# One block with adaptive norm, cached attention and a gated feed-forward: first pair's statistics on ScalarE, plane sums and scaling on GpSimd, first product copied, norm steps in order, seven split weights

## The chip, the cores and the metric

The kernel runs on one core of one Trainium2 chip. The core has five engines that are told apart in the profile: PE (TensorE, with its weight loads as PEld), DVE (VectorE), ACT (ScalarE), POOL (GpSimd) and SP (SyncE, which here issues DMAs). The metric is device microseconds of one execution; the time given is the median of the runs.

## The reference, cut to what matters

```python
x = A_x                                                   # 2048 tokens, 576 channels
sa, ca, ga, sb, cb, gb = silu(c) @ w_mod                  # six rows of 576
h = layernorm(x) * (1 + ca) + sa
x = x + ga * attention(h, k_cache, v_cache, wq, wo)       # 32 heads of 128, 16 kv heads, last 512 keys
h = layernorm(x) * (1 + cb) + sb
x = x + gb * ((sigmoid(h @ w_gate) * (h @ w_up)) @ w_down)  # 4608 hidden channels
```

Everything is float32. A product of two float32 matrices is made of three matmuls: each operand is split into a high part that PE takes whole and the remainder (`hi` and `lo`), and hi*lo, lo*hi and hi*hi are summed in PSUM (function `three`).

## The kernel before

Tokens are cut into four blocks of 512 (`xs[0..3]`, 128 partitions x 4 tiles x 576). There are three stages.

**Attention (0 to 1437 us).** A loop over 512 steps (`n`, one step for each tile of 128 queries of a head) issues projection matmuls (`qp`), scores (`st<-kt,qt`), transposes of the probabilities (`st<-ident,pp`) and value products (`ot<-ptt,vs`). DVE takes the negated maximum (`neg`), subtracts the low parts (`ptt`, `qt`) and scales the output (`ov<-ot,rb`); ACT makes the exponentials (`pp`) and high parts. Work for later stands beside it: `at_n(n, ...)` puts a function at a step. In this way the norm of blocks 2 and 3 (`norm_block`, L648), which the second half of the attention reads, is spread over steps near the middle, and the weights of the later stages are prepared in the background (`bg_load`, `bg_sums`, `bg_split`, `bg_store`): they are read into "rooms", which are the tiles of `xs` not in use, summed on POOL, split on ACT and POOL and written to DRAM. A loop at L812 plans the steps of these jobs by when a room comes free. `shift_cols` (L855) turns a row into columns by PE transposes. For the last two blocks of queries the reciprocal sums are spread over partitions by `spread_rs` (four diagonal tiles `dg` on DVE) and `spread_mm` (four matmuls with ones, then an ACT copy to `rb`).

**Output projection (1437 to some 1820 us).** 32 "visits", one for each tile of 128 tokens, pair of blocks and group of weights; the blocks of a pair are multiplied together by a scheme of seven products in place of eight. A visit has seven stages (`STAGES`) of 12 matmuls of 128x288. Its left operands are four planes `vr` loaded from DRAM and three sums of them (`vt`, made by `v_sum`, one of which overwrites a plane); each is split by `v_split` into `vh` (ACT the high part, DVE the low part). After each stage DVE adds the PSUM bank (tags a, b, c) onto `x`. With visit 24 (`DONE0`) the first pair of blocks is complete, and from there its second norm runs beside the visits: `ln_stats` and the chain of small DVE steps in `ln_chain`, then `early_norm` on ACT, `early_scale` on POOL or DVE, `early_sum` on DVE.

**Feed-forward (some 1820 to 3079 us).** 36 units of hidden channels for each pair of blocks; a unit has seven products (`product`, L1162; `a<-hc,sw`, `b<-hc,sw`, `c<-hc,sw`) of seven matmuls of 128x512, and between them the down products (`w<-wh,hl`). Weights come ready from DRAM (`wsc`) by `load_w` into `sr` (4 buffers) and are split by `split_w` into `sw` (5 buffers): ACT copies the high part, and POOL and DVE take turns in subtracting the low part. Each product issues at its end one `split_w` and one `load_w`, and only then is its PSUM bank copied (`keep`). S2's product leaves bank a, ACT copies it to `g1` (`g<-a`), and S3's product, one further on, goes into the same bank. At units 4, 9, 14 and 19 `late_tile` makes the second norm of the second pair: DVE and POOL work, and five DMAs (`put`) that write the result to DRAM from SP's queue.

**Order.** A scheduler may reorder instructions that are not pinned; `pin` and `keep_order` hold an instruction to the program's order. Each engine then runs its own list in order. SP issues loads and stores in one list too: a store that waits for its data holds up each load behind it.

Of the kernel before, what the change touches and what calls it, by code (L numbers as in the profile page):

```python
# [44 lines left out]
def adaln_block_kernel(ctx: ExitStack, tc: tile.TileContext, x, k_cache, v_cache, wq, wo, w_gate, w_up, w_down,  # L45
# [146 lines left out]
    def ln_chain(b, both):  # L192
        sl = slice(0, 2) if both else slice(b % 2, b % 2 + 1)
        mv, y, v, a = [z[:, sl] for z in LN[b][2]]
        yi, vi = y.bitcast(I32), v.bitcast(I32)
        ops = [lambda: nc.vector.tensor_scalar(v, mv[:, :, :, 1], EPS, None, op0=OP.add),
# [6 lines left out]
        ops += [lambda: nc.vector.scalar_tensor_tensor(a, mv[:, :, :, 0], -1.0, y, op0=OP.mult, op1=OP.mult)]  # L203
# [281 lines left out]
    def expo(n):  # L485
# [159 lines left out]
    for b in range(NB):  # L645
        at_n(N - 48 + 4 * b, load_x, b)

    def norm_block(b, n_stats, n_apply, n_t, step, sc_, sh_, mul, add):  # L648
# [4 lines left out]
        for k in range(12):  # L653
            at_n(n_stats + TPB + k, ln_some, b, False, k, k + 1)
# [3 lines left out]
    norm_block(2, n1 - 35, n1 - 19, n1 - 14, 2, scale, shift, nc.gpsimd, nc.gpsimd)  # L658
# [10 lines left out]
    EX = {}  # L669
# [10 lines left out]
    def early_scale(t, b):  # L680
        h = xs[b][:, t, :]
        (nc.vector if b else nc.gpsimd).tensor_mul(h, h, rows2["scale"])

    def early_sum(t, k):
        if k == 0 and t % 2 == 0:
            for c in (T1, T2, T4):
                EX[c, t // 2] = hp.tile([P, 2, D2], F32, tag="ts", name="ex", bufs=6)
# [131 lines left out]
    while jobs or wide:  # L819
# [10 lines left out]
        for r in rooms:  # L830
            free[r] = n + {"ab": 10, "tail": 13}.get(kind, 12)
        at_n(n, bg_load, k, rooms)
        for part in range(2):
            at_n(n + 4 + part, bg_sums, k, part)
            if kind != "ab":
                at_n(n + 6 + part, bg_split, k, part)
        for part in range(4 if kind == "tail" else 1):
            at_n(n + (7 if kind == "ab" else 8) + part, bg_store, k, part)
        due = max(due, n - 2) + {"ab": 4.6, "tail": 7.6}.get(kind, 5.9)

# [13 lines left out]

    def shift_cols():  # L855
        row = rows2["shift"]
        p = ps_wo()
        for half in range(2):
            e = wp.tile([P, 4, TQ], F32, tag="hd", name="hd", bufs=1)
            n0 = half * D2  # L860
            pin(nc.gpsimd.tensor_copy(e, row[:, None, n0 + 2 * P : n0 + D2].to_broadcast([P, 4, TQ])))
            for k in range(3):
                src = row[0:1, n0 + k * P : n0 + (k + 1) * P] if k < 2 else e.rearrange("p q d -> p (q d)")[0:1]
# [4 lines left out]
    at_n(110, shift_cols)  # L868
# [43 lines left out]
    def v_sum(v, k):  # L912
# [3 lines left out]
        eng = nc.vector if v > DONE0 and k % 2 else nc.gpsimd  # L916
        if k == 0:
            eng.tensor_add(VSUM[v, 0], raw[2], raw[3])
        elif k == 1:
            eng.tensor_sub(raw[2], raw[0], raw[2])  # L920
        elif k == 2:
            eng.tensor_sub(VSUM[v, 2], VSUM[v, 0], raw[0])
        else:
            eng.tensor_sub(VSUM[v, 3], raw[1], VSUM[v, 2])
# [71 lines left out]
    def stage_half(pair, c, i):  # L996
        t = hp.tile([P, 2, D2], F32, tag="ts", name="ts", bufs=6)
# [61 lines left out]
    def split_w():  # L1059
# [4 lines left out]
        t = fpool["s"].tile([P, 5, P], F32R, tag="sw", name="sw", bufs=5)  # L1064
# [122 lines left out]
    def late_load(t):  # L1187
        LATE[t] = [hp.tile([P, 2, D2], F32, tag="ts", name=n, bufs=6).rearrange("p a d -> p (a d)")
# [31 lines left out]
    def beside(v, s):  # L1220
# [14 lines left out]
        if DONE0 - 4 < v <= DONE0 and s in (0, 2):  # L1235
            ln_stats(s // 2, v - DONE0 + 3)
# [4 lines left out]
        if 3 <= k < 10:  # L1241
            ln_some(0, True, 2 * (k - 3), 2 * (k - 2), True)
# [22 lines left out]
    for v in range(VISITS):  # L1265
        q, pair, t = VISIT[v]
        banks = {}
        for s, (plane, combo, tag, row, col) in enumerate(STAGES):
            fresh = tag not in banks
            if fresh:  # L1270
                banks[tag] = fpsum(tag, 2 if tag == "a" else 1, [P, BLK])[:, :D2]
            p = banks[tag]
# [5 lines left out]
            dst = xs[2 * pair + row][:, t, col * D2 : (col + 1) * D2]  # L1278
            nc.vector.tensor_add(dst, p, dst)
# [162 lines left out]
```

## Time and profile before

| | us |
|---|---|
| median of 3 runs | 3082.25 |
| lowest and highest run | 3081.03 and 3084.95 |
| the profiled execution: its own time | 3081.02 |
| its span in the profile | 3079.0 |
| PE busy | 3022.5 |
| DVE, ACT, POOL busy | 2190.9, 1680.2, 1641.9 |

All engines' instructions are put down to one line, L36, because a helper records each of them; so the profile is read by tile names. A row of the timeline gives start, duration, engine, operation, the tiles written and read, the shape and, in brackets, the idle time ahead of it with what ended it. A row of the windows gives the stretch, its length, then the busy time of PE, PEld, DVE, ACT and POOL with their counts, the granted TensorE clock, the share of the DMA engines and GB/s.

### The profile page before, as it was taken

What the parts mean: (1) busy time and instruction counts of PE and PEld (TensorE: products, weight loads), DVE (VectorE), ACT (ScalarE), POOL (GpSimd) and SP (SyncE); (2) the same over time, 40 slices, a digit from 0 to 9 for tenths busy, and PEclk for the clock granted to TensorE, in tenths of its full rate; (3) what the DMA queues carried; (4) which work ended last, traced back from release to release, by engine and by line L of the source; (5) the groups of instructions that cost most, each with busy time, mean ns of one, the idle gap of its engine ahead of it and who ended that gap; (6) DMA issues with size and microseconds to landing.
All of it is one profiled execution on the core that took longest, in us unless ns stands there. A gap on an engine that the chain in (4) does not pass through costs nothing.

```text
span 3079.0 us, 49150 instructions
## 1 busy us (share of the span) xinstructions
PE 3022.5 (98%) x16651; PEld 2600.9 (84%) x16651; DVE 2190.9 (71%) x3872; ACT 1680.2 (55%) x3358; POOL 1641.9 (53%) x1534
## 2 busy tenths in 40 slices
PE   8999999999999999999999999999999999999998
PEld 6888788878888888887999888888888888888887
DVE  6666666677666666667888987666666876666667
ACT  5666666656667676554334454444544545444542
POOL 2334368644577773212555327666655666555654
PEclk9999999999999999999999999999999999999999
DMA  4687778766777777654546535555555564554453
GB/s 124 182 199 213 193 235 249 218 183 185 194 250 249 249 238 185 174 172 169 204 160 263 214 125 173 170 158 163 166 148 142 159 187 135 148 146 142 135 159 100
DMA packets 468795, 558.72 MB, mean 181 GB/s; under 512 B 51136, under 2 KB 421056, under 8 KB 459584
## 3 DMA queue, kind: packets, MB, share of 16 engines
q1 hardware_dynamic: 467408, 555.06, 60.1%
q8 instruction: 132, 2.16, 0.3%
q14 instruction: 119, 0.97, 0.1%
q10 hardware_dynamic: 1136, 0.53, 0.1%
HBM read 388.04 MB, written 167.41 MB: 180 GB/s over the span
## 4 chain that ended last, share of the span: by engine, by line
PE 87%; DVE 5%; POOL 3%; issue 2%; ACT 1%; DMA 1%; SPq 0%; POOLq 0%; ACTq 0%; DVEq 0%
PE a L36 19%; PE st L36 17%; PE qp L36 13%; PE w L36 12%; PE ot L36 11%; PE c L36 10%; PE b L36 5%; DVE x L36 1%; POOL x L36 1%; DVE vh L36 1%; POOL hl L36 0%; PE wo L36 0%; POOL vs L36 0%; DVE neg L36 0%; ACT pp L36 0%
## 5 line engine op out<-in xcount | busy, mean ns | idle before, releaser
L36 DVE TENSOR_TENSOR x<-w,x 128x288 f32<-128x288 f32 x980 | 435.6, 454 | 299.7 <-PE w L36 295.8
L36 PE MATMUL a<-hc,sw 128*128 128x512 f32 x2016 | 584.9, 395 | 9.2 <-POOL sw L36 5.2
L36 DVE TENSOR_REDUCE neg<-st 128x1 f32<-128x512 f32 x512 | 352.7, 689 | 281.1 <-PE st L36 281.1
L36 ACT ACTIVATE ptt<-st 128x512 fp32r<-128x512 f32 x512 | 306.2, 598 | 394.3 <-PE st L36 393.9
L36 PE MATMUL ot<-ptt,vs 128*128 128x512 f32 x1536 | 487.2, 425 | 2.9 <-DVE ptt L36 2.9
L36 PE MATMUL qp<-hTm,wa 128*128 128x512 f32 x1536 | 446.1, 399 | 4.9 <-DVE qt L36 2.8
L36 PE MATMUL st<-kt,qt 128*128 128x512 f32 x1536 | 443.0, 395 | 1.4 <-ACT pp L36 1.4
L36 DVE TENSOR_TENSOR ptt<-st,ptt 128x512 fp32r<-128x512 f32 x512 | 352.2, 688 | 123.4 <-ACT ptt L36 123.0
L36 ACT ACTIVATE sw<-sr 128x384 fp32r<-128x384 f32 x504 | 261.7, 521 | 261.9 <-issue 91.3
L36 PEld LDWEIGHTS a<-hc,sw 128*128 128x128 f32 x2016 | 355.9, 188 | 51.0 <-POOL sw L36 6.5
L36 ACT ACTIVATE pp<-st,neg 128x512 f32<-128x512 f32 x512 | 350.8, 685 | 55.6 <-DVE neg L36 55.1
L36 POOL TENSOR_TENSOR sw<-sr,sw 128x256 fp32r<-128x256 f32 x252 | 195.0, 775 | 325.1 <-ACT sw L36 228.9
L36 PEld LDWEIGHTS qp<-hTm,wa 128*128 128x128 f32 x1536 | 284.2, 188 | 74.2 <-DVE qt L36 8.3
L36 PEld LDWEIGHTS w<-wh,hl 128*128 128x128 f32 x1776 | 299.3, 189 | 54.8 <-DVE x L36 6.0
L36 PEld LDWEIGHTS st<-kt,qt 128*128 128x128 f32 x1536 | 288.5, 189 | 66.6 <-ACT pp L36 2.4
L36 PE MATMUL w<-wh,hl 128*128 128x288 f32 x1776 | 332.9, 298 | 3.4 <-DVE x L36 3.3
L36 POOL TENSOR_TENSOR x<-x 128x256 f32<-128x256 f32 (+3 forms) x334 | 246.9, 758 | 152.0 <-DMA x<-in_B_w_up_dram 88.4
L36 PEld LDWEIGHTS st<-ident,pp 128*128 128x128 f32 x2048 | 255.8, 140 | 78.0 <-issue 7.2
L36 PE MATMUL st<-ident,pp 128*128 128x128 f32 x2048 | 307.9, 273 | 9.2 <-DVE rs L36 6.4
L36 PE MATMUL c<-hc,sw 128*128 128x512 f32 x1008 | 303.8, 394 | 0.0
L36 PEld LDWEIGHTS ot<-ptt,vs 128*128 128x128 f32 x1536 | 253.5, 191 | 29.7 <-DVE ptt L36 4.2
L36 POOL TENSOR_TENSOR hl<-vs,hl 128x512 fp32r<-128x512 f32 x139 | 186.7, 1343 | 98.9 <-ACT hl L36 98.9
(211 smaller groups left out, 5107.1 us busy)
## 6 DMA issues: line engine op xcount, KB each, us to landing
sr<-wsc SPq DMA_DIRECT2D x504, 192.0 KB
wh<-dsc SPq DMA_DIRECT2D x144, 288.0 KB
dsc<-x SPq DMA_DIRECT2D x34, 1008.0 KB
vr<-oscr SPq DMA_DIRECT2D x32, 1024.0 KB
rb<-rscr SPq DMA_DIRECT2D x126, 256.0 KB
wsc<-x SPq DMA_DIRECT2D x36, 896.0 KB
oscr<-ov SPq DMA_DIRECT2D x63, 512.0 KB
wosc<-x SPq DMA_DIRECT2D x32, 1008.0 KB
```

Of the source, the lines that this page charges most:

```text
L36: i = got(*args, **kw)
```

## The change

- The small steps of the norm chain of blocks 2 and 3 are pinned, and block 2's statistics and application stand one step later.
- `spread_mm` is one matmul of 128x512 in place of four of 128x128, and stands one step later for the last but one block and two for the last.
- The two POOL copies that `shift_cols` needs are made ahead of it, at steps 100 and 101, into two buffers; the transposes stand at step 106 instead of 110.
- Background jobs hold their rooms one step longer, with the second half of a split and the stores one step later; the last reloads of `x` wait for the rooms.
- In each visit ACT copies the first product's bank into bank b, where the sixth product is then accumulated; the DVE add after the first product goes.
- The first pair's statistics move from DVE's `bn_stats` to ACT: three passes for each tile (a sum, its scaling to the negated mean, and the sum of squares about it), at visits 21 to 24.
- From visit 25 all of `v_sum` is on POOL (two of four were on DVE), and all of `early_scale` too.
- `sw` has seven buffers instead of five, `sr` three instead of four, `ts` four instead of six; two of the sums of `early_sum` lie in `sw` buffers. Three weights are loaded ahead, five are split beside the visits, and unit 1 has one more split and load.

```diff
-    def ln_chain(b, both):
-        sl = slice(0, 2) if both else slice(b % 2, b % 2 + 1)
-        mv, y, v, a = [z[:, sl] for z in LN[b][2]]
+    def chain(first, v, y, a, last):
...
-                at_late(n - 1, spread_mm, b)
+                at_late(n + (0 if b == NBLK - 2 else 1), spread_mm, b)
...
     def spread_mm(b):
         p = ps_qp()
-        for i in range(TPB):
-            nc.tensor.matmul(p[:, i * P : (i + 1) * P], ones, DG[b][:, i], start=True, stop=True)
+        nc.tensor.matmul(p, ones, DG[b].rearrange("p i q -> p (i q)"), start=True, stop=True)
...
-            at_n(n_stats + TPB + k, ln_some, b, False, k, k + 1)
+            at_n(n_stats + TPB + k, ln_some, b, False, k, k + 1, True)
...
-    norm_block(2, n1 - 35, n1 - 19, n1 - 14, 2, scale, shift, nc.gpsimd, nc.gpsimd)
+    norm_block(2, n1 - 34, n1 - 18, n1 - 14, 2, scale, shift, nc.gpsimd, nc.gpsimd)
...
+    def early_stats(b, t):
...
+        pin(nc.scalar.activation(junk, x, AF.Copy, accum_out=sums))
+        pin(nc.scalar.activation(means, sums, AF.Copy, scale=-1.0 / D))
+        pin(nc.scalar.activation(junk, x, AF.Square, bias=means, accum_out=squares))
...
-        (nc.vector if b else nc.gpsimd).tensor_mul(h, h, rows2["scale"])
+        nc.gpsimd.tensor_mul(h, h, rows2["scale"])
...
-            free[r] = n + {"ab": 10, "tail": 13}.get(kind, 12)
+            free[r] = n + {"ab": 10, "tail": 14}.get(kind, 13)
...
-                at_n(n + 6 + part, bg_split, k, part)
+                at_n(n + 6 + 2 * part, bg_split, k, part)
...
+    def shift_ends(half):
+        e = ends2[half] = wp.tile([P, 4, TQ], F32, tag=f"hd{half}", name="hd", bufs=1)
...
-    at_n(110, shift_cols)
+    for half in range(2):
+        at_n(100 + half, shift_ends, half)
+    at_n(106, shift_cols)
...
-        eng = nc.vector if v > DONE0 and k % 2 else nc.gpsimd
...
-            t = fpool["s"].tile([P, 3, P], F32, tag="sr", name="sr", bufs=4)
+            t = fpool["s"].tile([P, 3, P], F32, tag="sr", name="sr", bufs=3)
...
-        t = fpool["s"].tile([P, 5, P], F32R, tag="sw", name="sw", bufs=5)
+        t = fpool["s"].tile([P, 5, P], F32R, tag="sw", name="sw", bufs=7)
...
-            ln_stats(s // 2, v - DONE0 + 3)
+            early_stats(s // 2, v - DONE0 + 3)
...
-            for _ in range(4):
+            for _ in range(3):
                 load_w(True)
-        if k in (36, 39, 42, 45):
+        if k in (35, 38, 41, 44, 46):
             split_w()
             load_w(True)
...
+                if s == 0:
+                    banks["b"] = fpsum("b", 1, [P, BLK])[:, :D2]
...
-            dst = xs[2 * pair + row][:, t, col * D2 : (col + 1) * D2]
-            nc.vector.tensor_add(dst, p, dst)
+            if s == 0:
+                pin(nc.scalar.activation(banks["b"], p, AF.Copy))
+            else:
+                dst = xs[2 * pair + row][:, t, col * D2 : (col + 1) * D2]
+                nc.vector.tensor_add(dst, p, dst)
...
+        if u == 1:
+            split_w()
+            load_w()
```

**Three places in the order of instructions.** The first is DVE's list in the middle of the attention, where the norm of blocks 2 and 3 runs (`ln_a`, `ln_y` are the chain's small tiles, `h` a normed tile). Before:

```order
L36 SCALAR_TENSOR_TENSOR ln_a<-ln_a,ln_v 128x4
L36 SCALAR_TENSOR_TENSOR ln_y<-ln_a,ln_y 128x4
L36 TENSOR_TENSOR ln_a<-ln_y 128x4
L36 SCALAR_TENSOR_TENSOR ln_a<-ln_a,ln_v 128x4
L36 SCALAR_TENSOR_TENSOR ln_y<-ln_a,ln_y 128x4
L36 TENSOR_REDUCE neg<-st 128x1
L36 TENSOR_TENSOR ptt<-st,ptt 128x4x128
```

And with the change, where the same part of block 3's chain stands:

```order
L36 SCALAR_TENSOR_TENSOR ln_y<-ln_a,ln_y 128x4
L36 TENSOR_TENSOR ln_a<-ln_y 128x4
L36 TENSOR_REDUCE neg<-st 128x1
L36 TENSOR_TENSOR ptt<-st,ptt 128x4x128
L36 TENSOR_TENSOR ov<-ot,rb 128x4x128
L36 SCALAR_TENSOR_TENSOR qt<-qp,qt 128x512
L36 TENSOR_REDUCE neg<-st 128x1
L36 TENSOR_TENSOR ptt<-st,ptt 128x4x128
L36 SCALAR_TENSOR_TENSOR ln_a<-ln_a,ln_v 128x4
L36 SCALAR_TENSOR_TENSOR ln_y<-ln_a,ln_y 128x4
L36 TENSOR_REDUCE neg<-st 128x1
```

Five chain steps that stood in one run now stand in runs of two, with the attention's `neg` and `ptt` between.

The second is POOL's list in the visits after the first pair is complete (`x_101` and `x_102` are the first pair's blocks). Before:

```order
L36 TENSOR_TENSOR x_101<-x_101,scale_2199 128x576 x2
L36 COPY te<-x_101 128x256
L36 TENSOR_TENSOR x_101<-x_101,scale_2199 128x576
L36 TENSOR_TENSOR vt<-vr 128x512
L36 TENSOR_TENSOR vt<-vt,vr 128x512
L36 TENSOR_TENSOR x_101<-x_101,scale_2199 128x576
L36 COPY te<-x_101 128x256
```

With the change:

```order
L36 TENSOR_TENSOR x_101<-x_101,scale_2199 128x576
L36 COPY te<-x_101 128x256
L36 TENSOR_TENSOR x_102<-x_102,scale_2199 128x576
L36 TENSOR_TENSOR vt<-vr 128x512
L36 TENSOR_TENSOR x_101<-x_101,scale_2199 128x576
L36 TENSOR_TENSOR vr<-vr 128x4x128
L36 TENSOR_TENSOR x_102<-x_102,scale_2199 128x576
L36 TENSOR_TENSOR vt<-vt,vr 128x512
L36 TENSOR_TENSOR vt<-vr,vt 128x512
L36 TENSOR_TENSOR x_101<-x_101,scale_2199 128x576
```

The scaling of both blocks and four sums of a visit now stand in POOL's list, where there were one block and two sums.

The third is ACT's list in the feed-forward's unit 4, after the first `late_tile` (`v1`, `g0`, `g1` are copies of PSUM banks; numbers tell buffers apart, and the loads of `sr` come from SP in the order of their numbers). Before:

```order
L36 ACTIVATE v1_20550<-c_20445 128x512
L36 ACTIVATE g0_20468<-g0_20468 128x512
L36 ACTIVATE sw_20570<-sr_20466 128x384
L36 ACTIVATE g1_20575<-a_20443 128x512
L36 ACTIVATE sw_20596<-sr_20492 128x384
L36 ACTIVATE sw_20623<-sr_20523 128x384
L36 ACTIVATE g1_20575<-g1_20575 128x512
```

With the change:

```order
L36 ACTIVATE sw_20549<-sr_20470 128x384
L36 ACTIVATE v1_20554<-c_20449 128x512
L36 ACTIVATE g0_20472<-g0_20472 128x512
L36 ACTIVATE sw_20574<-sr_20496 128x384
L36 ACTIVATE g1_20579<-a_20447 128x512
L36 ACTIVATE sw_20600<-sr_20527 128x384
L36 ACTIVATE sw_20627<-sr_20552 128x384
L36 ACTIVATE g1_20579<-g1_20579 128x512
```

The list has the same shape, but each split takes a load one further on; SP's list shows where these loads are issued. Before, the loads on both sides of the writes of `late_tile` (`scr1`) are these:

```order
L36 DMA sr_20466<-wsc4_300 128x384
L36 DMA scr1_291<-h0_20216 128x2x288
L36 DMA wgate1_20486<-dsc1_333 128x2x288
L36 DMA scr1_291<-h1_20217 128x288
L36 DMA scr1_291<-tt_20218 128x2x288
L36 DMA scr1_291<-h1_20217 128x288
L36 DMA scr1_291<-h0_20216 128x288
L36 DMA sr_20492<-wsc5_301 128x384
```

With the change:

```order
L36 DMA sr_20470<-wsc5_301 128x384
L36 DMA scr1_291<-h0_20220 128x2x288
L36 DMA wgate1_20490<-dsc1_333 128x2x288
L36 DMA scr1_291<-h1_20221 128x288
L36 DMA scr1_291<-tt_20222 128x2x288
L36 DMA scr1_291<-h1_20221 128x288
L36 DMA scr1_291<-h0_20220 128x288
L36 DMA sr_20496<-wsc5_301 128x384
L36 DMA sr_20527<-wsc5_301 128x384
```

So the split that stands ahead of the copy `g1<-a` reads `sr_20466` before, which is loaded ahead of the five writes, and `sr_20496` with the change, which is loaded behind them.

More of the change, by code (lines that the diff above doesn't have):

```diff
@@ L202, in ln_chain @@
                     lambda: nc.vector.scalar_tensor_tensor(y, a, 1.5, y, op0=OP.add, op1=OP.mult)]
-        ops += [lambda: nc.vector.scalar_tensor_tensor(a, mv[:, :, :, 0], -1.0, y, op0=OP.mult, op1=OP.mult)]
+        return ops + [last]
+    def ln_chain(b, both):
+        sl = slice(0, 2) if both else slice(b % 2, b % 2 + 1)
+        mv, y, v, a = [z[:, sl] for z in LN[b][2]]
+        ops = chain(lambda: nc.vector.tensor_scalar(v, mv[:, :, :, 1], EPS, None, op0=OP.add), v, y, a,
+                    lambda: nc.vector.scalar_tensor_tensor(a, mv[:, :, :, 0], -1.0, y, op0=OP.mult, op1=OP.mult))
         for i in range(sl.start, sl.stop):
@@ L667, in park_x, with early_chain @@
         pin(nc.sync.dma_start(xscr[b][:, t], xs[b][:, t]))
-    EX = {}
+    EX, ES = {}, []
+    def early_stats(b, t):
+        if not ES:
+            ES.extend(const.tile([P, 2, TPB], F32, tag=f"es{i}", name=f"es{i}") for i in range(6))
+            for i in range(2):
+                LN[i], NMR[i] = [None, ES[4][:, i]], ES[5][:, i]
+        sums, means, squares = [e[:, b, t : t + 1] for e in ES[:3]]
+        x = xs[b][:, t, :]
+        junk = hp.tile([P, 2, D2], F32, tag="ts", name="junk", bufs=4).rearrange("p c d -> p (c d)")
+        pin(nc.scalar.activation(junk, x, AF.Copy, accum_out=sums))
+        pin(nc.scalar.activation(means, sums, AF.Copy, scale=-1.0 / D))
+        pin(nc.scalar.activation(junk, x, AF.Square, bias=means, accum_out=squares))
+    def early_chain():
+        sums, means, squares, v, y, a = ES
+        return chain(lambda: nc.vector.tensor_scalar(v, squares, 1.0 / D, EPS, op0=OP.mult, op1=OP.add),
+                     v, y, a, lambda: nc.vector.tensor_mul(a, means, y))
     def halves_of(b, t):
```

38 lines of the change are left out of this document (23 added, 15 removed).

## The prediction

> **What bounds the kernel now.** I read first the page's busy times, then what PE waits for in all, then the busy time by stage, then the timeline at each of the longer waits.
>
> ```profile
> PE 3022.5 (98%) x16651; PEld 2600.9 (84%) x16651; DVE 2190.9 (71%) x3872; ACT 1680.2 (55%) x3358; POOL 1641.9 (53%) x1534
> PE st L36 <- DVE rs L36: 6.4, 1, 6.4
> PE a L36 <- POOL sw L36: 5.2, 3, 1.7
> PE qp L36 <- DVE dg L36: 2.9, 5, 0.7
> PE wo L36 <- POOL hd L36: 1.0, 1, 1.0
> 1437.00:1704.00 267.00, 265.73 (x1983) 264.83 (x1984) 227.92 (x346) 103.64 (x165) 143.30 (x93) 0.99 0.56 208
> 1704.00:1800.00 96.00, 85.38 (x613) 81.79 (x612) 87.77 (x158) 39.91 (x64) 31.74 (x24) 1.00 0.48 177
> ```
>
> PE is busy 3022.5 of the span of 3079.0 us, so at most 56 us of it can be saved by anything that does not take matmuls away, and the change takes none away that costs PE time (below). What can be had lies in single waits. Two stretches of the output projection stand beside each other: in the early visits PE is idle 1.27 of 267 us with DVE busy 227.92 (85%); from 1704 to 1800 it is idle 10.62 of 96 with DVE busy 87.77 (91%). So DVE holds PE back in the late visits and nowhere for long otherwise. The profiled execution took 3081.02 us, 1.2 below the median of 3082.25; I add up against the former.
>
> **The change part by part.**
>
> *Norm steps in order.* DVE and PE at 659 to 666 us:
>
> ```profile
> 659.45 1.36 DVE L36 SCALAR_TENSOR_TENSOR ln_a<-ln_a,ln_v 128x4 f32<-128x4 f32 x1
> 662.20 0.16 DVE L36 TENSOR_TENSOR ln_a<-ln_y 128x4 f32<-128x4 f32 x1
> 663.68 1.18 DVE L36 SCALAR_TENSOR_TENSOR ln_y<-ln_a,ln_y 128x4 f32<-128x4 f32 x1
> 664.79 0.68 DVE L36 TENSOR_REDUCE neg<-st 128x1 f32<-128x512 f32 x1
> 660.76 1.39 POOL L36 TENSOR_TENSOR h<-h,scale 128x576 f32<-128x576 f32 x1
> 666.21 1.09 PE L36 MATMUL st<-ident,pp 128*128 128x128 f32 x4 [6.40 <-DVE rs L36]
> ```
>
> Five chain steps on 128x4 stand in one run ahead of `neg`. One takes 0.16 us when nothing disturbs it and 1.2 to 1.4 while POOL works on `h`; the run lasts from 659.45 to 664.79, and PE idles 6.40 behind it. Pinned, the chain has one or two steps at a time, with `neg` and `ptt` between, so no run of 5 us can form. POOL's work on `h` is still beside block 3's chain, so a disturbed step of 1.36 can still be late. All of the wait gone is -6.4; five such steps each in PE's way again, 5 x 1.2 = 6.0, is about 0. I take -5.5, nearer to the whole, because a single step of 1.36 is far shorter than the run.
>
> *Columns.* The POOL copies `hd` are made 5 steps before the transposes that read them. That is the wait of 1.0 above: -1.0, between -1.3 and 0. The cover is these five steps, of 1437 / 512 = 2.8 us each.
>
> *Reciprocals at the end of the attention.*
>
> ```profile
> 1421.34 3.22 DVE L36 TENSOR_SCALAR dg<-ident,rs 128x128 f32<-128x128 f32 x4
> 1424.61 0.49 PE L36 MATMUL qp<-dg,ones 128*128 128x128 f32 x2 [0.73 <-DVE dg L36]
> 1435.43 0.94 PE L36 MATMUL qp<-dg,ones 128*128 128x128 f32 x6 [0.73 <-DVE dg L36]
> 1438.27 4.37 PE L36 MATMUL ot<-ptt,vs 128*128 128x512 f32 x12 [1.90 <-DVE ptt L36]
> ```
>
> One matmul of 512 columns does the work of four of 128, and passes as many columns through PE: I count that at nothing (two of 128 last 0.49 us here; three of 512 last 0.85 in a row further down). PE waits 2.9 us for `dg` in all and 1.90 behind ACT's late `ptt` at 1438.27, because ACT's copy `rb` stands ahead of it. One or two steps later `dg` is ready. All gone is -4.8. `ov` is then late instead, and through `oscr` the planes of the visits that read it; the last wait may merely move there. I take -3, between -4.8 and 0.
>
> *The visits.* DVE and POOL from 1704 to 1800, and two ACT prices from the whole output projection and feed-forward:
>
> ```profile
> L36 DVE TENSOR_TENSOR vh<-vr,vh 128x512 fp32r<-128x512 f32 x31 | 24.8, 800 | 1.9 <-ACT vh L36 1.7
> L36 DVE TENSOR_TENSOR vr<-vr 128x512 f32<-128x512 f32 x7 | 5.8, 831 | 3.5 <-POOL vt L36 3.5
> L36 DVE TENSOR_TENSOR vt<-vr,vt 128x512 f32<-128x512 f32 x7 | 5.1, 735 | 0.2
> L36 DVE TENSOR_TENSOR x<-a,x 128x288 f32<-128x288 f32 x29 | 13.0, 449 | 0.4 <-PE a L36 0.4
> L36 DVE TENSOR_TENSOR x<-x,scale 128x576 f32<-128x576 f32 x4 | 3.0, 746 | 0.0
> L36 POOL TENSOR_TENSOR vt<-vr,vt 128x512 f32<-128x512 f32 x1 | 1.6, 1615 | 0.1
> L36 DVE TENSOR_TENSOR vh<-vr,vh 128x512 fp32r<-128x512 f32 x93 | 94.1, 1012 | 5.5 <-ACT vh L36 4.5
> L36 ACT ACTIVATE v<-c 128x512 f32<-128x512 f32 x72 | 43.1, 599 | 119.3 <-PE c L36 119.3
> L36 ACT ACTIVATE x<-x,ln_a,ln_y 128x576 f32<-128x576 f32 x8 | 6.7, 856 | 2.1 <-DVE ln_a L36 2.1
> ```
>
> The seventh row is that of 1437 to 1704. DVE loses in the late stretch: the sums 5.8 + 5.1, the scaling 3.0, and one add in seven (a visit is 267 / 24 = 11.1 us, so 8 visits x 0.449 = 3.6): 87.8 - 17.5 = 70.3 us; the last of its statistics, which go too, I leave out. It gains where POOL disturbs it more: the low parts `vh` take 1012 ns in the early visits, where POOL is busy 143.30 of 267, against 800 here: 31 x 0.21 = 6.6. So DVE comes to 77 of 96 (80%), under the 85% at which the early visits feed PE. At their rate of idling (1.27 / 267) 96 us hold 0.5 idle, so the stage saves 10.62 - 0.46 = -10.2. POOL goes from 31.74 to some 31.74 + 14 x 1.6 + 4 x 1.6 = 60.5 of 96, which the early visits bear in kind (54%).
>
> ACT takes on a copy of 128x288 from PSUM to PSUM for each visit. No row shows one; the nearest is `v<-c`, 128x512 from PSUM, at 0.60: I take 0.6 as its upper bound, once in a visit, hidden, as ACT is busy 103.64 of 267 there. It takes on the statistics too: two passes of 0.856 and a small one for each of 8 tiles at visits 21 to 24. A `vh` behind them comes later by up to 0.86. DVE's part of `vh` waits then, and PE after it, where the three `vh` buffers give no cover: I take +1 in all, between 0 and 8 x 0.86 = +7. So the visits: -9.2, between -10.2 and -1.
>
> *The attention's order.* The background jobs move by a step, and in PE's list four places are newly out of their usual rhythm of scores, transposes and values. Two such places of now:
>
> ```profile
> 193.60 0.63 PE L36 MATMUL st<-ident,pp 128*128 128x128 f32 x4 [0.33 <-DVE ptt L36]
> 839.82 0.50 PE L36 MATMUL st<-kt,qt 128*128 128x512 f32 x1 [1.21 <-ACT pp L36]
> ```
>
> Four at 0.33 to 1.21: +1.3 to +4.8. I take +2, with 0 below, since not each such place stalls PE.
>
> *Seven split weights.* The three waits of PE for `sw`, 5.2 us, all come behind a load that SP issued late. The first of them, and the ACT and PE rows of the other two:
>
> ```profile
> 1891.69 1.08 SPq L36 DMA_DIRECT2D scr<-h  x2
> 1892.87 4.32 SPq L36 DMA_DIRECT2D sr<-wsc  x3
> 1890.19 0.60 ACT L36 ACTIVATE g<-a 128x512 f32<-128x512 f32 x1 [0.96 <-PE a L36]
> 1895.44 1.00 ACT L36 ACTIVATE sw<-sr 128x384 fp32r<-128x384 f32 x2 [4.65 <-DMA sr<-wsc]
> 1892.36 0.85 PE L36 MATMUL a<-hc,sw 128*128 128x512 f32 x3
> 1896.90 0.73 PE L36 MATMUL a<-hc,sw 128*128 128x512 f32 x2 [1.72 <-POOL sw L36]
> 2066.85 1.02 ACT L36 ACTIVATE sw<-sr 128x384 fp32r<-128x384 f32 x2 [4.62 <-DMA sr<-wsc]
> 2063.80 0.85 PE L36 MATMUL a<-hc,sw 128*128 128x512 f32 x3
> 2487.74 1.03 ACT L36 ACTIVATE sw<-sr 128x384 fp32r<-128x384 f32 x2 [4.34 <-DMA sr<-wsc]
> 2484.57 0.85 PE L36 MATMUL a<-hc,sw 128*128 128x512 f32 x3
> L36 ACT ACTIVATE sw<-sr 128x384 fp32r<-128x384 f32 x504 | 261.7, 521 | 261.9 <-issue 91.3 <-ACT hl L36 39.8 <-DMA sr<-wsc 32.6
> ```
>
> SP issues the next weight at 1892.87, behind the writes of `late_tile`; its split starts at 1895.44, after ACT has copied `g1` (1890.19). PE runs on until it lacks that weight, 1.72 us. With two more split weights in hand PE no longer lacks one: -5.2. But the split that stands in ACT's list AHEAD of `g1<-a` now is the one whose load comes behind the writes. `g1<-a` frees bank a for S3's product, due at 1892.36. If the load lands as now, ACT splits at 1895.44, for 0.52, then copies for 0.60: PE can go on at 1896.56, 4.20 late. In the same way 2066.85 + 1.12 - 2063.80 = 4.17 and, at the change of pairs where SP writes `out`, 2487.74 + 1.12 - 2484.57 = 4.29: +12.7. Together +7.5, between -5.2 (the load comes early after all) and +9. At `late_tile` 1 and 3 the same split is late by about 1 us only, and the copy has 1892.36 - 1890.79 = 1.6 in hand. Six buffers `ts` becoming four can hold back the second pair's staging by one piece, +1.5 at the most; I take 0.
>
> Sum: -5.5 - 1.0 - 3 - 9.2 + 2 + 7.5 = -9.2, so 3081.02 - 9.2 = 3071.8; with the profiled run a little under the median I say **3072 us**.
>
> **The rivals.** *The weights come in time* (0.22): the load behind the writes lands before ACT reaches the split, so that the deeper splits give their -5.2 and no wait at `g1`. For it: DVE and POOL have less to do at other times, and two loads more lie split. Against it: the five writes wait for POOL's work on `h` and `tt`, which the change does not touch. -9.2 - 12.7 = -21.9: 3059.
>
> *POOL holds DVE in the late visits* (0.17): 18 more POOL instructions of 1.6 us there, 29 us; if each keeps a DVE instruction back for its whole length, DVE has 70.3 + 29 = 99 us for 96, and the stage saves nothing but what I allow as -1. For it: the chain steps of 1.36 in place of 0.16 above, and 1012 against 800 ns of `vh`. Against it: the early visits run so with PE fed. 3071.8 + 8.2 = 3080.
>
> The Trainium skill, page "SBUF — State Buffer", section "Who interferes with whom", has a rule that speaks against moving these sums: a DVE instruction with two SBUF inputs contends with a GpSimd instruction that reads SBUF, and the second to start is blocked until the first is through. By it nearly each `vh` would meet a POOL sum and this rival's 3080 would be the time. The trace agrees that such pairs disturb each other, but only in part: 800 ns of `vh` with POOL 33% busy and 1012 with 54%, not blocked for a whole sum each time.
>
> *ACT is held at more places* (0.13): of the 32.6 us that ACT's splits wait for loads now, 4.65 + 4.62 + 4.34 = 13.6 are the three above and 19.0 lie elsewhere, hidden. With one load fewer in `sr`, each of these too can come to stand ahead of a copy that frees a PSUM bank. All of them on PE's path are +19.0: 3091. From 16.6 of the 19.0 on the change is slower (3088.4). For it: the loads ahead of the split fall from four to three. Against it: most of the 261.9 ahead of the splits is no wait for a load, and two more split weights lie between a late load and PE.
>
> *The chain is held up as before* (0.06): pinned steps still meet POOL one after another. No -5.5: 3077.
>
> **How the numbers follow.** My forecast has 0.42, the rivals 0.22, 0.17, 0.13 and 0.06. The forecast's own range goes from 3066 to 3078. Two tenths left out, the range reaches down past 3059, to 3057, and up to 3088, most of the way to 3091. A difference under 0.2%, 6.2 us, can't be told from none: faster is under 3076.1, slower over 3088.4. Faster: nine tenths of 0.42, 0.22, and some 0.05 of the others, 0.65. Slower: most of 0.13, and a little of the rest, 0.15. Same: 0.20.
>
> **What would show it.** Right: no PE wait over 2 us at 650 to 680; PE idle under 2.5 us in the late visits with DVE near 80%; no PE wait for `sw` by POOL, but three of some 4 us for ACT `g` at the first and third `late_tile` and the change of pairs, each with a wait of ACT for `sr` ahead of it. Wrong: these three missing (3059); PE waits for DVE `x` and `vh` at the late visits as before, with DVE over 88% (3080); PE waits for ACT `g` or `v` at ten places or more (3091). A wait at the statistics of visits 21 to 24 over 3 us would break the term that I took as +1.

## The result: 13 us slower, in the feed-forward and the visits

| | before | changed |
|---|---|---|
| median of 5 runs, us | 3082.75 | 3096.05 |
| lowest and highest | 3081.03 and 3086.33 | 3091.03 and 3098.1 |
| ratio to before | | 1.0038, 95% interval 1.0024 to 1.0053 |
| span of the profiled execution | 3079.0 | 3094.2 |
| attention | 1441.3 | 1439.6 |
| output projection (visits) | 374.5 | 379.2 |
| feed-forward | 1256.2 | 1267.8 |

The three lower rows are of the profiled execution alone and are worked out from the starts of matmuls in its trace: from PE's first to the first that reads `vh`, from there to the first of `a<-hc,sw`, and on to PE's last. The forecast was 3072 us, range 3057 to 3088; the time is over the range. The attention is 1.7 us shorter, the visits 4.7 longer, the feed-forward 11.6 longer.

The busy times and PE's longest waits of the changed kernel (a wait: us in all, times, longest):

```profile
PE 3030.0 (98%) x16639; PEld 2599.0 (84%) x16639; DVE 2160.5 (70%) x3798; ACT 1700.2 (55%) x3430; POOL 1680.2 (54%) x1552
```

```profile
PE a L36 <- ACT g L36: 11.9, 3, 4.0
PE qp L36 <- DVE qt L36: 6.5, 4, 4.0
PE c L36 <- DVE x L36: 3.4, 1, 3.4
PE qp L36 <- DVE dg L36: 3.4, 2, 2.7
```

The wait for `rs` (6.4) and those of `a` for POOL's `sw` (5.2) are gone, and so is that for POOL's `hd`. In their place stand three waits for ACT's `g` of 4 us each and one of 4.0 for `qt`. PE is busy 7.5 us longer than before although it has 12 records fewer: that is not more work.

**Feed-forward.** ACT, SP and PE of the changed kernel at the first `late_tile`:

```profile
1893.24 0.62 ACT L36 ACTIVATE g<-g 128x512 f32<-128x512 f32 x1
1900.41 0.52 ACT L36 ACTIVATE sw<-sr 128x384 fp32r<-128x384 f32 x1 [6.54 <-DMA sr<-wsc]
1900.84 0.58 ACT L36 ACTIVATE g<-a 128x512 f32<-128x512 f32 x1
1896.69 1.09 SPq L36 DMA_DIRECT2D scr<-h  x2
1897.87 4.50 SPq L36 DMA_DIRECT2D sr<-wsc  x3
1897.14 0.40 PE L36 MATMUL c<-hc,sw 128*128 128x512 f32 x1
1901.47 1.65 PE L36 MATMUL a<-hc,sw 128*128 128x512 f32 x3 [3.93 <-ACT g L36]
1903.63 1.19 PE L36 MATMUL a<-hc,sw 128*128 128x512 f32 x3
1906.37 0.86 PE L36 MATMUL a<-hc,sw 128*128 128x512 f32 x3
```

SP issues the weight at 1897.87, behind the writes; ACT's split waits 6.54 us for it, the copy `g<-a` comes right behind the split, and PE, which could have gone on at 1897.5, waits 3.93 for the copy. This is the step that the prediction worked out to 4.20. What it left out stands in the same row: three matmuls that last 0.85 us elsewhere take 1.65 after the wait, and 1.19 still 2 us on; at 1906 they have their length again. The windows of the changed kernel in which the first, second and third such wait end (the last figure but two of a row is the granted clock):

```profile
1895.00:1905.00 10.00, 6.07 (x26) 5.00 (x25) 2.12 (x5) 1.42 (x3) 7.64 (x9) 0.83 0.46 141
2075.00:2085.00 10.00, 8.08 (x31) 6.95 (x32) 6.11 (x12) 4.23 (x9) 4.83 (x6) 0.66 0.65 222
2500.00:2510.00 10.00, 7.08 (x24) 6.03 (x25) 5.14 (x10) 3.40 (x7) 5.40 (x7) 0.66 0.80 245
```

Each long wait is paid twice: some 4 us of idling, and 1.5 to 2.6 us of slower matmuls behind it (the sum, over the 14 us that follow, of what each start-to-start step lasts beyond its median).

**Visits.** The changed kernel's window over the stretch that the prediction spoke of, and DVE's groups in it:

```profile
1704.00:1800.00 96.00, 82.56 (x574) 79.68 (x574) 83.19 (x120) 43.78 (x81) 56.78 (x41) 0.95 0.47 175
```

```profile
L36 DVE TENSOR_TENSOR x<-a,x 128x288 f32<-128x288 f32 x20 | 9.0, 451 | 2.6 <-PE a L36 2.6
L36 DVE TENSOR_TENSOR ex<-x,ex 128x288 f32<-128x288 f32 x8 | 8.1, 1009 | 0.0
L36 DVE TENSOR_TENSOR ex<-x,x 128x288 f32<-128x288 f32 x4 | 4.8, 1202 | 0.0
L36 DVE TENSOR_TENSOR x<-x 128x288 f32<-128x288 f32 x4 | 3.9, 971 | 0.0
```

The same groups before:

```profile
L36 DVE TENSOR_TENSOR ex<-x,ex 128x288 f32<-128x288 f32 x8 | 4.6, 574 | 0.0
L36 DVE TENSOR_TENSOR ex<-x,x 128x288 f32<-128x288 f32 x4 | 3.0, 753 | 0.0
L36 DVE TENSOR_TENSOR x<-x 128x288 f32<-128x288 f32 x4 | 1.8, 447 | 0.0
```

DVE does 38 instructions fewer and is still busy 83 us of 96: sums with both operands in SBUF take 1009, 1202 and 971 ns in place of 574, 753 and 447. The adds `x<-a,x`, whose one operand is a PSUM bank, keep their time (449 before, 451 now). The sixteen sums of the three groups take 16.8 us together in place of 9.4. PE idles 13.4 us in place of 10.6, and the clock falls to 0.95. The timeline shows where: POOL's eight scalings run from 1728.86 to 1750.80 with plane sums between, and in that stretch PE waits 2.32, 3.42 and 2.07 us.

**Attention.** DVE, SP and PE of the changed kernel at the norm:

```profile
656.02 1.05 DVE L36 TENSOR_TENSOR ov<-ot,rb 128x512 f32<-128x512 f32 x1
667.11 1.05 DVE L36 TENSOR_TENSOR ov<-ot,rb 128x512 f32<-128x512 f32 x1 [3.96 <-DMA rb<-rscr]
657.10 0.57 SPq L36 DMA_DIRECT2D oscr<-ov  x1
657.72 0.63 SPq L36 DMA_DIRECT2D rscr<-rs  x1
661.87 0.34 SPq L36 DMA_DIRECT2D rb<-rscr  x1
657.13 3.07 PE L36 MATMUL ot<-ptt,vs 128*128 128x512 f32 x12 [0.15 <-DVE ov L36]
668.88 1.65 PE L36 MATMUL qp<-hTm,wa 128*128 128x512 f32 x3 [3.96 <-DVE qt L36]
```

No run of chain steps stands in DVE's list any more. But an `ov` stands late in that list, at 656.02. The value matmuls come in one piece of twelve right behind it, at 657.13 (the 0.15 is their wait for it). SP's store of `ov`, at 657.10, holds up the store of `rs` behind it, although DVE had made an `rs` at 645.6 that no store had taken yet. So `rb` comes back late, and the next `ov` waits 3.96 for it with `qt`, which PE needs, behind.

### The profile page after: what moved, and what is told of

Read it like the earlier page. It is cut to its first block, busy times and chain, and to the rows that moved or that the text cites. A ratio compares the mean times of both kernels' runs of the same rounds, so it can differ in the third digit from the quotient of the medians.

```text
span 3094.2 us, 49195 instructions
## 1 busy us (share of the span) xinstructions
PE 3030.0 (98%) x16639; PEld 2599.0 (84%) x16639; DVE 2160.5 (70%) x3798; ACT 1700.2 (55%) x3430; POOL 1680.2 (54%) x1552
## 4 chain that ended last, share of the span: by engine, by line
PE 88%; DVE 4%; POOL 2%; DMA 2%; issue 1%; ACT 1%; SPq 0%; ACTq 0%; POOLq 0%; DVEq 0%
PE a L36 20%; PE st L36 18%; PE qp L36 13%; PE w L36 12%; PE ot L36 11%; PE c L36 10%; PE b L36 5%; DVE x L36 1%; DMA sr<-wsc 1%; POOL hl L36 1%; POOL x L36 1%; POOL vs L36 0%; DVE neg L36 0%; PE wo L36 0%; DMA wh<-wosc 0%
## 5 line engine op out<-in xcount | busy, mean ns | idle before, releaser
L36 POOL TENSOR_TENSOR sw<-sr,sw 128x256 fp32r<-128x256 f32 x252 | 206.6, 820 | 306.9 <-ACT sw L36 303.5
L36 POOL TENSOR_TENSOR x<-x,x 128x1152 fp32r<-128x1152 f32 (+1 forms) x100 | 191.1, 1916 | 112.8 <-ACT x L36 88.5
```

Of the source, the lines that this page charges most:

```text
L36: i = got(*args, **kw)
```

## The experiments

Each kernel was timed five to eleven times, against the kernel before on the same chip; ratios are to before, with their 95% intervals. Stage lengths are made as above, each from one execution, and they scatter: the attention has the same order of instructions in the changed kernel and in runs 1, 3, 4, 5, 7 and 8, and takes 1438.4 to 1442.4 us in these seven executions. The visits are the same in the changed kernel and in runs 1, 6, 7 and 8, and take 377.4 to 379.2.

**1. The copy ahead of the split.** In the changed kernel:

```diff
     def product(u, a, c, p, first, downs=(2, 5), copy=None):
...
+        kept = copy() if copy else None
-        split_w()
+        split_w(copy is not None)
         load_w()
...
-        product(u, S2, T2, pa, False, downs)
-        g1 = keep(pa, "g1", 1)
+        g1 = product(u, S2, T2, pa, False, downs, lambda: keep(pa, "g1", 1))
```

(with the copy and that split pinned).

> The changed kernel with one edit: after S2's product ACT's copy of bank a to g1 is pinned ahead of the weight split, so that the copy no longer stands behind a split that waits for its load. Theory A (the copy is held by the split): the three PE waits for ACT g (11.9 us in all) go, and with them the lower granted clock behind each (0.66 to 0.83 in the 10 us after it): 12 to 18 us less, about 3080. Rival B (PE lacks the weight itself, the copy only stands in the way): the waits come back as waits for sw of 1.7 us or more at the same three places, 5 to 7 us less, about 3090.

Measured: 3095.87 us, 1.0044 (1.003 to 1.0057). No wait for ACT's `g` is left, and the time is that of the changed kernel. PE's two longest sums of waits in this run, and its DVE and PE at the first place:

```profile
PE a L36 <- DVE v L36: 13.0, 8, 3.6
PE w L36 <- DVE x L36: 8.7, 9, 2.3
```

```profile
1899.61 0.78 DVE L36 TENSOR_TENSOR sw<-sr,sw 128x256 fp32r<-128x256 f32 x1 [6.37 <-ACT sw L36]
1900.31 0.81 DVE L36 TENSOR_TENSOR x<-w,x 128x288 f32<-128x288 f32 x2
1900.81 0.67 PE L36 MATMUL w<-wh,hl 128*128 128x288 f32 x3 [2.32 <-DVE x L36]
```

Neither theory had this. The late weight holds not only ACT but DVE: every second low part is a DVE instruction, it waits 6.37 us for ACT's split, and the adds behind it, which free the down products' banks, wait with it. PE waits 2.32 us for such an add and 1.39 for DVE's `v` behind it, together 3.71 in place of 3.93. The copy was the first thing in the way and not the only one.

**2. The seven split weights alone**, on the kernel before:

```diff
-            t = fpool["s"].tile([P, 3, P], F32, tag="sr", name="sr", bufs=4)
+            t = fpool["s"].tile([P, 3, P], F32, tag="sr", name="sr", bufs=3)
-        t = fpool["s"].tile([P, 5, P], F32R, tag="sw", name="sw", bufs=5)
+        t = fpool["s"].tile([P, 5, P], F32R, tag="sw", name="sw", bufs=7)
```

(with the change's loads, splits and smaller `ts`).

> The kernel before with only the seven split weights (sw 7 buffers, sr 3, ts 4, two sums in sw buffers, five splits ahead, one more at unit 1). Theory A: three PE waits for ACT g of about 4 us take the place of three waits for sw of 1.7, with a lower clock behind them: 7 to 13 us slower than before. Rival B (the waits for ACT g need the later arrival of POOL's work in the changed visits): no more than 2 us slower.

Measured: 3100.83 us, 1.0056 (1.0044 to 1.0069), 18 us over before by the medians; the feed-forward of its profiled execution is 1269.0 against 1256.2. Its waits:

```profile
PE a L36 <- ACT g L36: 11.7, 3, 3.9
```

The same three waits come from this part by itself. The size is over what theory A allowed by the medians (13), and within it by the stage (12.8).

**3. Plane sums and scaling back on DVE**, in the changed kernel:

```diff
+        eng = nc.vector if v > DONE0 and k % 2 else nc.gpsimd
-            nc.gpsimd.tensor_sub(raw[2], raw[0], raw[2])
+            eng.tensor_sub(raw[2], raw[0], raw[2])
...
-        nc.gpsimd.tensor_mul(h, h, rows2["scale"])
+        (nc.vector if b else nc.gpsimd).tensor_mul(h, h, rows2["scale"])
```

> The changed kernel with two of the four sums of a late visit and the scaling of the second block on DVE again; the copy of the first product and the statistics on ACT stay. Theory A (POOL's work on two SBUF operands holds DVE): PE idle from 1704 to 1800 falls from 13.4 to 3 to 6 us, the kernel 8 to 12 us faster than the changed one, about 3086. Rival B (the statistics and the copy on ACT delay vh): the idle stays over 11 and the time within 3 us of the changed one.

Measured: 3089.56 us, 1.0019 (1.001 to 1.0028). The visits are 373.2 us against 379.2, and 374.5 before. Runs **4 and 5** did the scaling alone and the sums alone:

> The changed kernel with only the scaling of the second block on DVE again. Theory A (the scaling blocks: four instructions of 1.6 us in a row of eight from 1729 to 1751, beside DVE's sums of two operands from SBUF): most of the 6 us that both edits together gave in the visits, PE idle in 1704 to 1800 from 13.4 to 9 or less. Rival B (the plane sums do it): under 2 us.

> The changed kernel with only two of the four plane sums of a late visit on DVE again. Theory A (the scaling blocks): under 2 us gained in the visits, or none. Rival B (the plane sums on POOL come too late or hold DVE): 4 to 6 us gained, PE idle in 1704 to 1800 from 13.4 to 9 or less.

Measured: 3093.01 us, 1.0034 (1.0021 to 1.0046) and 3090.45 us, 1.0025 (1.0015 to 1.0035), visits 375.9 and 375.1. The window of 1704 to 1800 in run 3, in 4 and in 5:

```profile
1704.00:1800.00 96.00, 86.88 (x622) 84.07 (x621) 81.18 (x146) 46.77 (x84) 30.79 (x25) 0.98 0.48 175
```

```profile
1704.00:1800.00 96.00, 84.92 (x600) 82.22 (x599) 85.33 (x129) 45.07 (x83) 51.64 (x37) 0.96 0.48 175
```

```profile
1704.00:1800.00 96.00, 85.98 (x606) 83.03 (x605) 81.50 (x139) 46.98 (x87) 38.82 (x29) 0.96 0.48 175
```

PE idles 9.1 us with both, 11.1 with the scaling and 10.0 with the sums back, against 13.4 in the changed kernel. Moving work to POOL did cost the time, as theory A of run 3 has it, but 4.3 us of idling came back and not 7 to 10, and 6.5 us of the time by the medians and not 8 to 12. Each half gives part of it: of the 6.0 us of the visits, 3.3 come back with the scaling and 4.1 with the sums. The theories of 4 and 5 both asked for one culprit and both fell. DVE's busy time is 81.2 to 85.3 in all of them; what differs is how much POOL has there (30.8 to 56.8). The sums go the same way in the kept traces: the mean of the eight `ex<-x,ex` is 1009 ns in the changed kernel, 868 with the scaling back, 712 with the sums back and 584 with both, and `x<-a,x` stays at 450 to 451 in all four. So that these DVE instructions last longer beside more POOL work is shown. Some of PE's waits there are for ACT (`vh` 1.0 and 0.8, `sw` 1.9 in the changed kernel), and the runs do not divide the 6.0 us among the waits.

**6. Background jobs at the old steps**, in the changed kernel:

```diff
-            free[r] = n + {"ab": 10, "tail": 14}.get(kind, 13)
+            free[r] = n + {"ab": 10, "tail": 13}.get(kind, 12)
-                at_n(n + 6 + 2 * part, bg_split, k, part)
+                at_n(n + 6 + part, bg_split, k, part)
-            at_n(n + (7 if kind == "ab" else 9) + part, bg_store, k, part)
+            at_n(n + (7 if kind == "ab" else 8) + part, bg_store, k, part)
```

> The changed kernel with the background jobs' steps as before (rooms held one step less, split and store at the old steps). Theory A (the planner's new steps make the scheduler gather twelve value matmuls at 657 us, and the wait of DVE for rb of 3.96 follows from that): no wait of PE over 1.5 us between 650 and 680, 5 to 8 us faster than the changed kernel, about 3090. Rival B (the norm region stalls in any order): a PE wait of 4 to 6 us there again, within 2 us of the changed kernel.

Measured: 3090.24 us, 1.0023 (1.0013 to 1.0034); attention 1437.0 against 1439.6. The twelve value matmuls in one piece are gone from PE's list and no wait over 0.4 us is left between 650 and 680 us; one of 2.26 for `qt` stands at 634. One pair of executions is too few for the size: the four with this order in the attention (runs 6, 9, 11 and 12) take 1430.9 to 1437.0 there, 1434.3 on average, and the seven with the changed kernel's order 1439.7 on average. That is 5.4 us, and the medians of the whole time lie 5.8 apart. The steps of jobs that touch no instruction of the attention decided in which order the scheduler put the attention's own.

**7. Six split weights and four raw ones**, in the changed kernel:

```diff
-            t = fpool["s"].tile([P, 3, P], F32, tag="sr", name="sr", bufs=3)
+            t = fpool["s"].tile([P, 3, P], F32, tag="sr", name="sr", bufs=4)
-        t = fpool["s"].tile([P, 5, P], F32R, tag="sw", name="sw", bufs=7)
+        t = fpool["s"].tile([P, 5, P], F32R, tag="sw", name="sw", bufs=6)
-            for _ in range(3):
+            for _ in range(4):
-        if k in (35, 38, 41, 44, 46):
+        if k in (36, 39, 42, 45):
```

> The changed kernel with six split buffers and four raw ones in place of seven and three (four loads ahead, four splits beside the visits and one at unit 1). The split that stands ahead of g1 after S2's product then reads a weight whose load is issued ahead of the five writes again. Theory A (one raw buffer too few puts a late load ahead of the copy): the three PE waits for ACT g of 4 us go, other waits of under 1 us at those places: the feed-forward 10 to 14 us shorter, some 3083. Rival B (the split weights in hand are what counts, and six are too few): waits for sw of 1 us and more are back, less than 8 us gained.

Measured: 3077.71 us, 0.9983 (0.9974 to 0.9992), 18 us under the changed kernel; the feed-forward is 1251.6, 16.2 shorter than in the changed kernel and 4.6 shorter than before. Its ACT at the first `late_tile`:

```profile
1890.02 0.52 ACT L36 ACTIVATE sw<-sr 128x384 fp32r<-128x384 f32 x1
1890.74 0.60 ACT L36 ACTIVATE g<-a 128x512 f32<-128x512 f32 x1 [0.20 <-PE a L36]
1898.21 0.52 ACT L36 ACTIVATE sw<-sr 128x384 fp32r<-128x384 f32 x1 [6.45 <-DMA sr<-wsc]
```

ACT still waits 6.45 us for a late load, but behind the copy, and PE has enough split weights to work on until 1901. What is left there is a wait of 1.5 for DVE's `x`. One raw buffer more and one split buffer less turned the deeper splits from a loss into a gain. Runs 9 to 12 have the same feed-forward and take 1252.0 to 1254.7 us there, so the gain over before is some 1.5 to 4.6 us, where the prediction had counted on 5.2 from the waits for `sw`.

**8. The writes from POOL's queue**, in the changed kernel:

```diff
-            nc.sync.dma_start(d[:, c : c + v.shape[1], :], v)
+            nc.gpsimd.dma_start(d[:, c : c + v.shape[1], :], v)
```

> The changed kernel with late_tile's five writes issued from POOL's queue instead of SP's; nothing else is changed. Theory A (the writes wait for POOL's results and hold the weight loads behind them in SP's list): the waits at the first and third late_tile (1897 and 2072 us) go, the one at the change of pairs (2498) stays: 10 to 12 us faster than the changed kernel, some 3085. Rival B (the load is late because the DMA engines are busy, or because a raw buffer comes free late): both waits stay over 2 us, within 3 us of the changed kernel.

Measured: 3105.61 us, 1.0072 (1.0059 to 1.0084), the slowest of all. At the first place PE's wait for ACT's `g` is gone, and one of 7.39 us for DVE's `v` has come, 7.4 again at the third `late_tile`. PE, SP and POOL of this run:

```profile
1909.31 1.65 PE L36 MATMUL a<-hc,sw 128*128 128x512 f32 x3 [7.39 <-DVE v L36]
1888.87 10.89 SPq L36 DMA_DIRECT2D sr<-wsc  x2
1897.33 0.56 POOL L36 DMA_DIRECT2D scr<-h  x1
1898.68 0.74 POOL L36 TENSOR_TENSOR sw<-sr,sw 128x256 fp32r<-128x256 f32 x1
1899.36 0.56 POOL L36 DMA_DIRECT2D scr<-h  x1
```

None of these writes stands in SP's list now, and the first of the two loads goes out at 1888.87, which is 9 us earlier than the load of 1897.87 in the changed kernel. The second is held until some 1899.4, when POOL's subtraction has read a raw buffer for the last time (1898.68 + 0.74). So a raw buffer that comes free late holds a load as well as a write does, and here later than in the changed kernel, since POOL issues the writes itself (0.56 to 0.88 us each) ahead of the subtraction. Theory A is right about what held the first load and wrong about what its freedom is worth. In the changed kernel the last read of a raw weight before that load is this one of POOL's:

```profile
1893.51 0.74 POOL L36 TENSOR_TENSOR sw<-sr,sw 128x256 fp32r<-128x256 f32 x1
```

From 1894.25 on no engine reads a raw weight until the load is issued, so its buffer was free by then, and the writes alone held it for the 3.6 us up to 1897.87. The third load of the same row, at 1902.06, is held by a buffer there too: POOL reads a raw weight from 1901.05 to 1902.03. Taking the writes out of SP's list frees the first load, and the next is then late through its buffer.

**9. The three edits together** (those of runs 3, 6 and 7):

> The changed kernel with three edits of the earlier runs together: six split and four raw buffers, the background jobs at the old steps, two plane sums and the second block's scaling on DVE. If the three losses are separate, their stage lengths add: attention 1437.0 (from the run with old steps), visits 373.2 (from the run with DVE's work back), feed-forward 1251.6 (from the run with six and four), against 1441.3, 374.5 and 1256.2 before: 10 us under before, about 3072. If they are one loss (the same lower clock seen three times), or one edit undoes another: over 3078.

Measured: 3071.78 us, 0.9957 (0.9945 to 0.997). Attention 1434.5, visits 373.0, feed-forward 1252.0: each within 2.5 us of the run that mended that stage. The losses are separate and add up, and this version, the mended kernel, beats both others. That it comes out at the 3072 of the forecast is chance: its visits gain 1.5 us where 9.2 were forecast. From it three parts of the change were undone, one at a time (**10, 11 and 12**). The norm's order:

```diff
-            at_n(n_stats + TPB + k, ln_some, b, False, k, k + 1, True)
+            at_n(n_stats + TPB + k, ln_some, b, False, k, k + 1)
-    norm_block(2, n1 - 34, n1 - 18, n1 - 14, 2, scale, shift, nc.gpsimd, nc.gpsimd)
+    norm_block(2, n1 - 35, n1 - 19, n1 - 14, 2, scale, shift, nc.gpsimd, nc.gpsimd)
```

> The mended kernel with the norm chain of blocks 2 and 3 unpinned and at its old steps. Theory A (order in the chain is worth its 6.40 us and the lower clock behind it): a PE wait of 6 us near 660 is back, attention 4 to 8 us longer than in the mended kernel. Rival B (the wait came from the other old steps): no such wait, within 2 us.

Measured: 3078.16 us, 0.9981 (0.9972 to 0.999); attention 1441.2 against 1434.5. The wait is back as it was:

```profile
PE st L36 <- DVE rs L36: 6.4, 1, 6.4
```

The statistics, on DVE again (here with its chain, too):

```diff
-            early_stats(s // 2, v - DONE0 + 3)
+            ln_stats(s // 2, v - DONE0 + 3)
```

> The mended kernel with the first pair's statistics on DVE (bn_stats) as before. Theory A (ACT's passes relieve DVE, which is busy 85% to 91% there): the visits 1 to 4 us longer than in the mended kernel. Rival B (ACT's passes delay vh as much as they relieve DVE): the same within 1 us, or shorter.

Measured: 3070.61 us, 0.9952 (0.994 to 0.9965), the lowest time of all, though not clear of the mended kernel's; the visits are 371.3 against 373.0. From 1704 to 1800 PE idles 9.4 us against 9.2; most of the 1.7 us lies in a stretch of slower matmuls behind a wait of 2.6, which came in one execution and not in the other (granted clock 0.98 there in the mended kernel, 1.00 here). ACT's passes relieve nothing that PE waits for. DVE's add after the first product:

```diff
-            if s == 0:
-                pin(nc.scalar.activation(banks["b"], p, AF.Copy))
-            else:
-                dst = xs[2 * pair + row][:, t, col * D2 : (col + 1) * D2]
-                nc.vector.tensor_add(dst, p, dst)
+            dst = xs[2 * pair + row][:, t, col * D2 : (col + 1) * D2]
+            nc.vector.tensor_add(dst, p, dst)
```

> The mended kernel with DVE's add after the first product of a visit in place of ACT's copy into bank b. Theory A (one DVE instruction of 0.45 less in each of 32 visits relieves the late ones): the visits 2 to 4 us longer than in the mended kernel. Rival B (DVE's time there is set by waits for POOL, not by the adds): the same within 1 us.

Measured: 3074.49 us, 0.9971 (0.9959 to 0.9982); visits 375.3 against 373.0. From 1704 to 1800 PE idles 11.5 us against 9.2. The copy is worth some 2.3 us in the visits and is the part of their change that pays; the whole times lie 2.7 apart by the medians, and their intervals overlap.

## Why the prediction was wrong, step by step

| step | forecast, us | measured, us | from |
|---|---|---|---|
| norm steps in order | -5.5 | -6.7 | attention of runs 9 and 10 |
| columns | -1.0 | -1.0 | PE's wait for `hd`, gone |
| reciprocals | -3 | some 0 | see below |
| visits | -9.2 | +4.7 | visits |
| attention's order | +2 | +5.4 | attention, means of the seven and the four executions of run 6 |
| seven split weights | +7.5 | +11.6 | feed-forward |

The measured steps come to +14.0 us, and the medians lie 13.3 apart.

- **The visits are the step that failed**, by 14 us. The prediction took 70.3 us of work for DVE, 6.6 for disturbance, and called 80% busy enough because the early visits feed PE at 85%; so PE was to idle 0.5 us from 1704 to 1800. It idled 13.4, with DVE busy 83.2 (87%). The 6.6 counted the low parts `vh` alone, which came out as forecast (1021 ns, forecast 1012); the 7.4 us by which the sums `ex` and `x<-x` lengthen stand nowhere in it, although they too have both operands in SBUF. The 60.5 us that it gave POOL are 63% of 96, more than the 54% of the early visits that it called alike. And it looked at an average over 96 us. The work that moved is not spread: eight scalings and four sums stand in one stretch of 22 us, and the sums on two SBUF operands, which take 1.6 to 2.2 times their time over the 96 us, stand there one behind the other. The price was in the rival *POOL holds DVE in the late visits*, which had 0.17 and gave the stage no gain; even that was too kind, since three waits over 2 us close together brought the lower clock.
- The Trainium skill, page "SBUF — State Buffer", section "Who interferes with whom", says that it is DVE instructions with two SBUF inputs that are held by GpSimd's reads. The rows of the changed kernel agree, and more sharply than the prediction granted: `ex` and `x<-x` take 1.6 to 2.2 times as long, `x<-a,x` from a PSUM bank does not move.
- **Seven split weights: the mechanism was right, the size was off.** Three waits for `g` at the three places named, 3.93 us at the first where 4.20 was forecast. The term left out what a wait of 4 us does to the matmuls behind it, 1.5 to 2.6 us each. The bound of +9 was too low for the same reason. Shorter waits that it put at nothing came too: 0.87 after the fourth `late_tile` (3 in the prediction, which counts from 0) and three of 0.42 to 0.52 ahead of the first.
- **Norm in order** was right in place and near in size, which only the mended kernel shows; the forecast left out the slower matmuls behind the 6.40. In the changed kernel a new wait of 3.96 stood in its place, so that the sign *no PE wait over 2 us at 650 to 680* failed.
- **The attention's order** was right in sign only: it cost more than twice the 2 us, and by one wait through SP's list with slower matmuls behind it, not by four small ones.
- **Reciprocals.** One matmul, placed later, still waits 0.74 for the first `dg` and 2.67 for the second, where waits of 0.15 to 0.73 and of 1.90 were: from 1400 to 1437 us PE is busy 33.2 before and 33.1 now. What is late is DVE's four `dg`, which take 3.0 and 2.9 us as before (3.22 and 2.70); the edit does not touch them.
- **The statistics on ACT**, put at +1, held nothing up: from 1437 to 1704 us PE is busy without a break.

## What to carry to other kernels

When a weight's split waits for its load in an engine's list, count what stands behind it on every engine that touches the weight, and choose how many raw and split buffers there are by which load is still ahead of the slowest write, not by the sum of both kinds. Judge an offload in the stretch where its instructions will stand together, and by instruction pairs that share an operand's memory, since an average of busy time over the stage hides both. In these traces a PE wait of 3.4 us or more costs more than its length.

## What the runs showed of the hardware

After long waits of PE its matmuls run 1.8 times as long for some 3 to 7 us. Waits of 4 us in the changed kernel are followed by steps at 1.83 to 1.89 times their median, and windows of 10 us with a granted clock of 0.66 to 0.83. Two windows of the kernel before, the first behind its wait of 6.40, the second around its wait of 1.90 at 1438:

```profile
665.00:675.00 10.00, 8.79 (x34) 7.29 (x35) 5.74 (x10) 5.09 (x12) 4.31 (x6) 0.67 0.30 54
1436.00:1448.00 12.00, 10.10 (x56) 9.01 (x55) 4.60 (x8) 2.67 (x5) 1.30 (x1) 0.86 0.79 267
```

In the traces of all fourteen kernels every wait of 3.4 us or more is followed by slower steps. Shorter ones go both ways. None of the waits of 1.70 to 1.75 in the kernel before is followed by them, the 1.90 at 1438 is, and one of 3.05 in run 1 is not. A wait of 1.85 for `hTm` at 23 to 25 us, which is in every kernel, is followed by them in seven executions and not in the other seven; where it is, 1.7 to 2.0 us are lost, which is part of why stage lengths scatter. Where several waits stand close together (2.32, 3.42 and 2.07 at 1735 to 1750) there are slow stretches too. The Trainium skill, page "TensorE: Matmul & The Clock Gate", section "Why this matters for your kernels", gives the limit as idle gaps of some 3 us between bursts of matmuls; above 3.4 us the rows agree with it, and below it they show slower matmuls after waits from 1.85 us on. The row of 6.40 showed this cost before the prediction was made, and it was not read.
